# A fused retention and MLP kernel: running state in SBUF, seven products for the first block too, and attention groups taken from a list

## Chip, cores, metric

One core of a Trainium2 chip. The metric is the device time of one execution in microseconds (us), median of the runs; lower is better. The profile's span (first to last instruction) is some 1.5 to 2.5 us shorter than that time. Ratios are the mean time of one kernel's fast runs over the mean of the other's of the same rounds, so they are not quite the ratios of the medians quoted beside them.

## The reference

```python
# q, k, v: (8, 8, 576, 64) float32; w_in: (512, 2048); w_out: (2048, 512)
scores = q @ k^T / sqrt(64)
ret    = scores * gamma_h ** (i - j)   for i >= j, else 0     # gamma_h = 1 - 2**(-5-h)
x      = (ret @ v), heads side by side                        # 4608 tokens x 512
out    = gelu_exact(x @ w_in) @ w_out                         # 4608 x 512, float32
```

## The kernel before

The engines are called as in the profile: PE does the matmuls (PEld its weight loads), DVE elementwise work, ACT copies and GELU, POOL here mostly issues loads. PSUM is the memory, in banks, that PE writes its sums to.

Attention goes by chunks: 8 sequences of 576 tokens, each four chunks of 128 and one of 64 tokens, 40 chunks in all. A chunk is turned (q and k transposed), `scores` gives k·q, DVE masks it, `inner` multiplies by v, `cross` adds what the state of all earlier chunks gives, `evacuate` writes x. The MLP goes by nine blocks of 512 tokens: a first layer (64 matmuls of 512 columns, GELU on ACT) and a second layer.

The program writes its instructions in a fixed order, which a modelled clock picks while the program is built. Each step has a rule for when it is ready; the step placed next is one that is ready by the modelled clock. On the chip each engine then runs its own instructions in that order, and the true semaphores make it wait where the model was wrong.

The second layer of blocks 1 to 8 is done by seven products in place of eight (112 matmuls of 256 columns for the work of 64 of 512). The products need sums of weights (`w_sum`, "T") and sums of g (`s`, "S"), made by DVE. Block 0 does its second layer plainly:

```python
    def mlp2_step(t, ts, m0, m1):              # block 0 only: out rows <- g, w_out tile by tile
        wait(land_out[(m1 - 1) // 2])          # modelled landing of THIS w_out tile
        wait(g_ready(t, ts * 128, ts * 128 + 128, range(m0, m1)))
        ...
    PRODUCTS = {1: ("A11", "B11", "P"), 2: ("A12", "B21", "Q"), 6: ("S2", "T2", "P"), 7: ("S3", "T3", "Q"),
                5: ("S1", "T1", "P"), 3: ("S4", "B22", "P"), 4: ("A22", "T4", "Q")}

    def fast_ready(t, n):                      # when a step of the seven products is ready
        k, p = (LAST_ORDER if t == N_BLK - 1 else FAST_ORDER)[n]
        lhs, rhs, where = PRODUCTS[k]
        ...                                    # sums s or g there, accumulator copied out, a bank free
        if rhs[0] == "T":
            when = max(when, w_sum_end[0])     # nothing is asked for rhs[0] == "B", the plain w_out
        return when

    def state(i):                              # sum over chunks kept in one PSUM bank
        ... matmul(u_ps[0][...], lhsT=k of chunk i, rhs=vh of chunk i, start=(ci == 0 and hp == 0), ...)
        nc.scalar.copy(u, u_ps[0])

    def attend(kind, i):                       # (cut) a pair of chunks: array modes 1, 2, 1
        if len(pend) == 2: state(pend[0])      # mode 1 (128x64)
        for j in pend: inner(j)                # mode 1
        for j in new:  scores(j)               # mode 2 (64x64)
        for j in pend: cross(j)                # mode 2
        if len(pend) == 2: state(pend[1])      # mode 1 again; the MLP's matmuls are mode 0 (128x128)
```

## Time and profile before

| | before |
|---|---|
| time, median of the runs | 298.8 us (298.5 to 299.1) |
| span of the profiled run | 296.9 us |
| PE busy | 288.6 us, 97% |
| DVE / ACT busy | 57% / 44% |
| matmul work done by 35 / 50 us | 19.4 / 33.2 us |

The last row is worked out from the trace: every matmul that has ended, taken at its steady rate (512 columns 0.2158 us, 256 columns 0.1092, 128 columns 0.0558), divided by the tiles that run side by side in its array mode, without warm-up matmuls. The whole program is 262.9 us of this.

Lines of the page of the kernel before: busy time with its share of the span, then PE, DVE and the granted PE clock in 40 slices of 7.4 us (tenths).

```profile
PE 288.6 (97%) x3151; PEld 192.8 (65%) x3151; DVE 169.1 (57%) x368; ACT 130.9 (44%) x259; POOL 113.8 (38%) x146
PE   6999999999999999999999999999999999999995
DVE  4652646947779726986089827581775144402422
PEclk9999999999999999999999999999999999999999
```

PE is busy from the second slice to the last but one, so only less PE work, fewer mode changes or a better start can shorten this. What PE does while the weights are still arriving matters below; this is its timeline there, start and duration in us, then the operation, its shape and count:

```profile
35.48 3.63 PE L435 MATMUL oT<-w_out,g 128*128 128x512 bf16 x16
38.95 0.61 PE L270 MATMUL qk_ps<-ident,qk_ld 128*128 128x128 bf16 x8
39.39 1.03 PE L435 MATMUL oT<-w_out,g 128*128 128x512 bf16 x4
40.35 0.42 PE L295 MATMUL sc<-qkT 64*64 64x128 bf16 x16
40.70 1.90 PE L435 MATMUL oT<-w_out,g 128*128 128x512 bf16 x8
...
43.34 3.63 PE L435 MATMUL oT<-w_out,g 128*128 128x512 bf16 x16
```

From 35 us on PE fills its time with `oT`, block 0's plain second layer.

The cost of a change of array mode is read from the chain of waits, here around one pair of chunks (start, us on the chain, what):

```profile
113.21 0.24 PE u_ps L351 x8
113.45 0.45 PE o_ps L331 x16
113.90 0.35 PE sc L295 x16
114.25 0.45 PE o_ps L370 x16
114.70 0.24 PE u_ps L351 x8
114.94 2.73 PE fast L535 x24
117.67 0.34 PE o_ps L331 x8
118.01 0.12 PE u_ps L351 x8
```

`u_ps x8` is 0.24 us when it opens a group (113.21) or comes behind another mode (114.70), and 0.12 behind `o_ps`, which is in its own mode (118.01): 0.12 us for a change. Walking all matmuls in order of time gives 112 changes.

### The profile page before, as it was taken

To read this page: it belongs to the slowest core of one execution; us is meant where nothing else is said; L and a number is where in the kernel's file an instruction comes from. 1 tells how busy PE (TensorE), PEld (TensorE's weight loads), DVE (VectorE), ACT (ScalarE), POOL (GpSimd) and SP (SyncE) were. 2 spreads that over 40 slices of the span, in tenths; PEclk is the share of its full clock that TensorE was granted. 3 is DMA by queue.
4 is the path that set the end of the run, shared out by engine and by line. 5 is a ranking of instruction groups with operands and counts; after the bars stand their busy time and mean duration, and the time that the engine had idled before them with its cause. 6 is when DMAs were issued, how large, how long until landed. Compare 5 with 4: busy or idle time off the path is not lost.

```text
span 296.9 us, 7431 instructions
## 1 busy us (share of the span) xinstructions
PE 288.6 (97%) x3151; PEld 192.8 (65%) x3151; DVE 169.1 (57%) x368; ACT 130.9 (44%) x259; POOL 113.8 (38%) x146
## 2 busy tenths in 40 slices
PE   6999999999999999999999999999999999999995
PEld 2675755658865488557864786568656864784584
DVE  4652646947779726986089827581775144402422
ACT  4676502655235613554246414651465146426621
POOL 8997879838485260690781075000000000000000
PEclk9999999999999999999999999999999999999999
DMA  9999999999999999999999999900300030003013
GB/s 92 152 182 176 190 187 187 199 144 131 155 147 202 166 155 149 210 157 166 77 230 137 134 78 223 162 10 3 141 2 2 0 143 0 2 5 137 3 35 106
DMA packets 153089, 35.48 MB, mean 119 GB/s; under 512 B 141792, under 2 KB 148960, under 8 KB 153056
## 3 DMA queue, kind: packets, MB, share of 16 engines
q0 software_dynamic: 117872, 18.23, 86.4%
q1 hardware_dynamic: 35184, 16.78, 31.9%
q8 instruction: 24, 0.39, 0.5%
q14 instruction: 9, 0.07, 0.1%
HBM read 36.70 MB, written 9.44 MB: 155 GB/s over the span
## 4 chain that ended last, share of the span: by engine, by line
PE 84%; DMA 7%; DVE 6%; POOL 2%; issue 1%; POOLq 0%; DVEq 0%
PE hT L403 38%; PE fast L535 32%; DMA v_ld<-in_v_dram 4%; PE sc L295 3%; PE o_ps L331 3%; PE o_ps L370 2%; PE oT L435 2%; PE u_ps L351 2%; DMA w_in<-in_moe_w_in_dram 2%; DMA qk_ld<-in_q_dram 1%; PE qk_ps L270 1%; DVE vh L316 1%; POOL qk_ld L185 1%; DVE s L468 1%; DVE qkT L273 1%
## 5 line engine op out<-in xcount | busy, mean ns | idle before, releaser
L403 PE MATMUL hT<-xT,w_in 128*128 128x512 bf16 (+7 forms) x692 | 130.2, 345 | 1.0 <-DVE xT L382 0.8
L409 ACT ACTIVATE g<-hT 128x512 bf16<-128x512 f32 (+6 forms) x173 | 89.5, 527 | 53.7 <-PE hT L403 50.9
L403 PEld LDWEIGHTS <-w_in 128*128 128x128 bf16 x692 | 62.0, 98 | 59.5 <-issue 0.9
L535 PEld LDWEIGHTS <-s 128*128 128x128 bf16 x512 | 49.6, 98 | 7.0 <-DVE s L468 0.8
L185 POOL DMA_DIRECT2D qk_ld<-in_q_dram x39 | 33.9, 869 | 47.1 <-DMA qkT<-qk_ld 39.9
L306 DVE TENSOR_TENSOR ret<-sc,msk 128x512 bf16<-128x512 f32 x64 | 41.1, 682 | 11.1 <-PE sc L295 10.7
L535 PE MATMUL fast<-w_sum,s 128*128 128x256 bf16 x384 | 43.8, 273 | 0.5 <-DVE s L468 0.5
L535 PEld LDWEIGHTS <-g 128*128 128x128 bf16 x384 | 37.5, 98 | 5.8
L185 POOL DMA_DIRECT2D v_ld<-in_v_dram x39 | 34.0, 871 | 12.9 <-DVE s L468 3.5
L559 DVE TENSOR_TENSOR o_sb<-fast,u 128x512 f32<-128x512 f32 (+1 forms) x18 | 11.4, 631 | 48.2 <-PE fast L535 39.2
L185 POOL DMA_DIRECT2D qk_ld<-in_k_dram x39 | 33.9, 869 | 5.6 <-DMA v_ld<-in_v_dram 4.4
L535 PE MATMUL fast<-w_out,g 128*128 128x256 bf16 x256 | 29.3, 273 | 0.0
L382 DVE TENSOR_TENSOR xT<-o_ps,dq 128x512 bf16<-128x512 f32 (+1 forms) x42 | 24.3, 605 | 7.4 <-PE o_ps L370 5.8
L467 DVE TENSOR_TENSOR s<-g 128x512 bf16<-128x512 bf16 x32 | 13.4, 420 | 25.0 <-ACT g L409 24.8
L555 ACT COPY u<-fast 128x512 f32<-128x512 f32 (+1 forms) x18 | 9.7, 538 | 39.9 <-PE fast L535 39.9
L356 ACT CAST u_sb<-u_ps 128x256 bf16<-128x256 f32 x32 | 11.9, 372 | 32.2 <-PE u_ps L351 32.1
L316 DVE TENSOR_TENSOR vh<-v_ld,dv 128x512 bf16<-128x512 bf16 x32 | 21.2, 680 | 6.4 <-DMA v_ld<-in_v_dram 6.4
L535 PE MATMUL fast<-w_out,s 128*128 128x256 bf16 x128 | 15.6, 272 | 0.0
L535 PE MATMUL fast<-w_sum,g 128*128 128x256 bf16 x128 | 15.3, 273 | 0.0
L435 PE MATMUL oT<-w_out,g 128*128 128x512 bf16 x64 | 15.2, 380 | 0.0
L295 PE MATMUL sc<-qkT 64*64 64x128 bf16 (+1 forms) x576 | 14.1, 223 | 0.5 <-ACT qkT L276 0.4
L468 DVE TENSOR_TENSOR s<-s,g 128x512 bf16<-128x512 bf16 x32 | 13.6, 425 | 1.1
(62 smaller groups left out, 192.6 us busy)
## 6 DMA issues: line engine op xcount, KB each, us to landing
out_dram<-o_sb SPq DMA_DIRECT2D x14, 512.0 KB, 4.7
qk_ld<-in_k_dram POOLq DMA_DIRECT2D x32, 128.0 KB, 7.3
v_ld<-in_v_dram POOLq DMA_DIRECT2D x32, 128.0 KB, 7.4
qk_ld<-in_q_dram POOLq DMA_DIRECT2D x31, 128.0 KB, 7.3
w_in<-in_moe_w_in_dram POOLq DMA_DIRECT2D x8, 256.0 KB, 6.8
w_out<-in_moe_w_out_dram POOLq DMA_DIRECT2D x8, 256.0 KB, 7.8
out_dram<-o_sb SPq DMA_DIRECT2D x4, 256.0 KB, 5.8
out_dram<-o_sb SPq DMA_DIRECT2D x8, 128.0 KB, 1.7
```

Of the source, the lines that this page charges most:

```text
L185: nc.gpsimd.dma_start(dst[:cs], src[b, :, c0:c0 + cs, :].rearrange("h s d -> s h d"))
L295: nc.tensor.matmul(sc[e][lo:lo + 64, hp, :cs], lhsT=qkT[sl, 1, hp, lo:lo + 64], rhs=qkT[sl, 0, hp, :cs], start=True, stop=True, skip_group ...
L306: nc.vector.tensor_tensor(r[:cs, :, :cs], sc[e][:cs, :, :cs], msk[:cs, :, :cs].to_broadcast([cs, HP, cs]), op=ALU.mult)
L316: nc.vector.tensor_tensor(vh[:cs], loaded[i][1][:cs], dv[:cs, :, ci:ci + 1].to_broadcast([cs, H, D]), op=ALU.mult)
L356: nc.scalar.copy(u, u_ps[0])
L382: nc.vector.tensor_tensor(xT[:, :, at:at + hi - lo], s["o_ps"][:, :, lo:hi], dq[:, :, c0 + lo:c0 + hi], op=ALU.mult)
L403: nc.tensor.matmul(hT[:, :hi - lo], lhsT=w[:, cc, o:o + 128], rhs=xT[:, cc, tok0 % RING + lo:tok0 % RING + hi], start=(cc == 0), stop=(cc ...
L409: nc.scalar.activation(g_of(t, m, lo, hi), hT[:, :hi - lo], AF.Gelu)
L435: nc.tensor.matmul(oT, lhsT=g_of(t, m, ts * 128, (ts + 1) * 128), rhs=w_out_sb[:, m // 2, m % 2, :], start=(m == 0), stop=(m == N_DF - 1))
L467: nc.vector.tensor_tensor(u[:, 0], a[2, 1], a[2, 2], op=ALU.add)
L468: nc.vector.tensor_tensor(u[:, 1], u[:, 0], a[1, 1], op=ALU.subtract)
L535: nc.tensor.matmul(acc_[:, p, :], lhsT=left(t, lhs, j, p), rhs=right(rhs, j), start=(fresh and j == 0 and (p == 0 or apart)), stop=(j == N ...
```

## The change

Intent: fewer array modes per pair, and one block more by seven products. The state of each chunk is made on its own, two to a bank, and added by DVE to a sum in SBUF, so that both states of a pair can stand in front of `inner` and a pair needs modes 1, 2 and 0. Block 0 goes by seven products; block 1's first layer, which could already be taken beside block 0's second, now goes first where both are ready. How many chunks to start, and when, comes from a list; the load order is another; chunk 9 is turned by DMA and no longer by PE.

```diff
-    N_PE_TR = 10
+    N_PE_TR = 9
+    LOADS = "1 2 i 3 i i 4 i o i i 5 i i 6 7 o o 8 o o o o o"   # digits: chunks, i: w_in, o: w_out
+    PLAN = [(1, 4), (0, 28), (1, 13), (1, 112), (0, 95), (1, 68), (1, 28), (1, 65), (0, 9), (2, 17), ... (0, 29)]
-    FAST_FROM = 1
+    FAST_FROM = 0
-    for what in "1 i 2 i i 3 z i i i i i 4 5 o o o o 6 o o o o 7 8".split():
+    for what in LOADS.split():
 ...
-    def state(i):
+    def states(upto):
+        ... u_ps, tag = bank([128, 2, HP, D], FP32, "u_ps")        # two chunks, each its own sum
+                if ci == 0:            nc.vector.tensor_copy(run_sum, u_ps[:, r])
+                elif ci < NCH - 2:     nc.vector.tensor_tensor(run_sum, run_sum, u_ps[:, r], op=ALU.add)
+                if ci < NCH - 2:       nc.scalar.copy(u, run_sum)
+                else:                  nc.vector.tensor_tensor(u, run_sum, u_ps[:, r], op=ALU.add)
 ...
-    def mlp2_step(t, ts, m0, m1):                  # removed, with its wait for each w_out tile
 ...                                                # fast_ready: still nothing asked for a plain w_out
+    stages = [first_runs[0], first_runs[1] + [second_run[0]], [second_run[0]] + first_runs[1], ...]
 ...
-            if len(pend) == 2: state(pend[0])
+                states(upto)
+                for j in pend: inner(j)
             for j in new: scores(j)
             for j in pend: cross(j)
-            if len(pend) == 2: state(pend[1])
```

More of the change, by code (lines that the diff above doesn't have):

```diff
@@ L54 @@
     N_RING = 4
-    LEAD = 44
-    PAIR_FROM = 2
-    PAIR_LEAD = 70
-    LATE_LEAD = 40
-    FAST_FROM = 1
+    LD_FIX = 2.5
+    LD_TAIL = 1.9
+    T_FIX = 2.4
+    T_TAIL = 4.2
+    T_DMA = 1.8
+    N_DYN = 3
+    LOADS = "1 2 i 3 i i 4 i o i i 5 i i 6 7 o o 8 o o o o o"
+    T_LEAD = 5
+    TR_LEAD = 5
+    PLAN = [(1, 4), (0, 28), (1, 13), (1, 112), (0, 95), (1, 68), (1, 28), (1, 65), (0, 9), (2, 17), (1, 82), (0, 51), (0, 53), (2, 2), (1, 0), (2, 56), (2, 18), (1, 0), (2, 52), (2, 36), (2, 71), (2, 0), (2, 89), (0, 89), (1, 145), (2, 127), (2, 119), (2, 135), (2, 98), (1, 76), (1, 129), (2, 216), (0, 29)]
+    FAST_FROM = 0
     HALF = TOK_BLK // 2
@@ L69 @@
     u_pool = ctx.enter_context(tc.tile_pool(name="u", bufs=4))
-    g_pool = ctx.enter_context(tc.tile_pool(name="g", bufs=1))
+    g_pool = ctx.enter_context(tc.tile_pool(name="g", bufs=2))
     s_pool = ctx.enter_context(tc.tile_pool(name="s", bufs=1))
@@ L99, in on_dve @@
         return on("DVE", ready, n / rate / 960 + 0.072)
-    first = o_pool.tile([128, d_model], FP32, tag="o_std", name="q32", bufs=4).rearrange("p (h d) -> p h d", d=D)
+    first = o_pool.tile([128, d_model], FP32, tag="m1", name="q32").rearrange("p (h d) -> p h d", d=D)
     nc.sync.dma_start(first, q[0, :, 0:C, :].rearrange("h s d -> s h d"))
@@ L135 @@
     nc.vector.memset(ones, 1.0)
+    ret_short = [const_pool.tile([128, HP, 128], BF16, name=f"ret_short{e}") for e in range(2)]
+    vh_short = const_pool.tile([128, H, D], BF16, name="vh_short")
+    for t in ret_short + [vh_short]:
+        nc.vector.memset(t, 0.0)
     diag = const_pool.tile([128, 128], BF16, name="diag")
@@ L159, with serve, transfer, load @@
     nc.scalar.activation(warm_act, ln_scale, AF.Gelu)
-    ret_short = [const_pool.tile([128, HP, 128], BF16, name=f"ret_short{e}") for e in range(2)]
-    vh_short = const_pool.tile([128, H, D], BF16, name="vh_short")
     loaded = {}
-    land_in, land_out = [], []
+    land_in, land_out = [None] * (N_DF // 2), [None] * (N_DF // 2)
     land_q, land_k, land_v = {}, {}, {}
-    dma_clock = [6.0]
-    def land(issue, took):
-        dma_clock[0] = max(dma_clock[0], issue) + took
-        return dma_clock[0]
+    rings = ([], [])
+    dma_at = [0.0]
+    pool_at = [3.3]
+    def serve(queues, t, until, landed):
+        while t < until:
+            heads = [q_[0] for q_ in queues if q_ and q_[0][0] <= t]
+            later = [q_[0][0] for q_ in queues if q_ and q_[0][0] > t]
+            if not heads:
+                if not later:
+                    return
+                t = min(later)
+                continue
+            rate = 1.0 / len(heads)
+            step = min([job[1] / rate for job in heads] + [x - t for x in later] + [until - t])
+            for job in heads:
+                job[1] -= step * rate
+            t += step
+            for q_ in queues:
+                if q_ and q_[0][1] < 1e-9:
+                    _, _, tail, at, key = q_.pop(0)
+                    if landed:
+                        at[key] = t + tail
+    def transfer(ring, start, took, tail, at, key):
+        serve(rings, dma_at[0], clock[0], True)
+        dma_at[0] = max(dma_at[0], clock[0])
+        rings[ring].append([start, took, tail, at, key])
+        ahead = tuple([list(job) for job in q_] for q_ in rings)
+        serve(ahead, dma_at[0], 1e5, True)
+    def load(took, at, key):
+        pool_at[0] = max(pool_at[0], clock[0]) + 0.87
+        transfer(0, pool_at[0] - 0.87 + LD_FIX, took, LD_TAIL, at, key)
     def load_chunk(i, now=0.0):
@@ L185, in load_chunk @@
             nc.gpsimd.dma_start(dst[:cs], src[b, :, c0:c0 + cs, :].rearrange("h s d -> s h d"))
-            at_[i] = land(now + 4.3, 0.88 * cs / C)
+            load(0.87 * cs / C, at_, i)
         loaded[i] = (qk, v_ld)
@@ L199, in load_w_in @@
         w_in_sb.append(t)
-        land_in.append(land(0.0, 1.36))
+        load(1.34, land_in, j)
     def load_w_out():
-        j = len(land_out)
+        j = next(j for j in range(N_DF) if land_out[j] is None)
         nc.gpsimd.dma_start(
@@ L206, in load_w_out @@
         )
-        land_out.append(land(0.0, 1.33))
+        load(1.34, land_out, j)
     load_chunk(0)
-    for what in "1 i 2 i i 3 z i i i i i 4 5 o o o o 6 o o o o 7 8".split():
+    for what in LOADS.split():
         if what == "i":
@@ L214 @@
             load_w_out()
-        elif what == "z":
-            for t in ret_short + [vh_short]:
-                nc.gpsimd.memset(t, 0.0)
         else:
@@ L221 @@
     st = {i: {} for i in range(N_CH)}
-    u_ps = [None]
+    run_sum = const_pool.tile([128, HP, D], FP32, name="run_sum")
     u_free = [0.0]
     mlp_begun = [False]
-    free_at = dict.fromkeys("abcdefg", 0.0)
+    free_at = dict.fromkeys("abcdefgh", 0.0)
     last_tag = [None]
@@ L246, in tiled @@
         if mode[0] != n:
-            clock[0] += 0.1
+            clock[0] += 0.115
         mode[0] = n
@@ L261, in turn @@
                               qk[:cs].rearrange("p j h d -> p (j h d)"), transpose=True)
-            dma_clock[0] = max(dma_clock[0], clock[0] + 3.0) + 1.8 * cs / C
-            s["turned"] = max(clock[0] + 9.0, dma_clock[0] + 1.5)
+            transfer(1, clock[0] + T_FIX, T_DMA * cs / C, T_TAIL, s, "turned")
             return
@@ L335, in inner @@
         s["o_end"] = clock[0] + SEEN
-    def state(i):
-        b, ci, c0, cs = chunks[i]
-        s = st[i]
-        if ci + 1 == NCH:
-            return
-        wait(s["scaled"])
-        wait(u_free[0])
-        tiled(1)
-        if ci == 0:
-            u_ps[0] = ps.tile([128, HP, D], FP32, tag="u", name="u_ps")
-        for hp in range(HP):
-            for e in range(2):
-                h = 2 * hp + e
-                nc.tensor.matmul(u_ps[0][64 * e:64 * e + 64, hp, :], lhsT=loaded[i][0][:cs, 1, h, :],
-                                 rhs=s["vh"][:cs, h, :], start=(ci == 0 and hp == 0),
-                                 stop=(hp == HP - 1), skip_group_check=True)
-        clock[0] += 0.125
-        u = st[i + 1]["u"] = u_pool.tile([128, HP, D], BF16, tag="u", name="u_sb")
-        nc.scalar.copy(u, u_ps[0])
-        u_free[0] = st[i + 1]["u_end"] = on_act(clock[0] + SEEN, 256) + BACK
+    def states(upto):
+        js = []
+        while nxt["U"] <= upto:
+            if chunks[nxt["U"]][1] + 1 < NCH:
+                js.append(nxt["U"])
+            nxt["U"] += 1
+        for n in range(0, len(js), 2):
+            some = js[n:n + 2]
+            for j in some:
+                wait(st[j]["scaled"])
+            tiled(1)
+            u_ps, tag = bank([128, 2, HP, D], FP32, "u_ps")
+            for r, j in enumerate(some):
+                for hp in range(HP):
+                    for e in range(2):
+                        h = 2 * hp + e
+                        nc.tensor.matmul(u_ps[64 * e:64 * e + 64, r, hp, :], lhsT=loaded[j][0][:C, 1, h, :],
+                                         rhs=st[j]["vh"][:C, h, :], start=(r == 0 and hp == 0), stop=(hp == HP - 1),
+                                         skip_group_check=True)
+                clock[0] += 0.125
+            ready = clock[0] + SEEN
+            for r, j in enumerate(some):
+                u = st[j + 1]["u"] = u_pool.tile([128, HP, D], BF16, tag="u", name="u_sb")
+                ci = chunks[j][1]
+                if ci == 0:
+                    nc.vector.tensor_copy(run_sum, u_ps[:, r])
+                    end = on_dve(max(ready, u_free[0]), 256) + BACK
+                elif ci < NCH - 2:
+                    nc.vector.tensor_tensor(run_sum, run_sum, u_ps[:, r], op=ALU.add)
+                    end = on_dve(max(ready, u_free[0]), 256) + BACK
+                if ci < NCH - 2:
+                    nc.scalar.copy(u, run_sum)
+                    u_free[0] = st[j + 1]["u_end"] = on_act(end, 256) + BACK
+                else:
+                    nc.vector.tensor_tensor(u, run_sum, u_ps[:, r], op=ALU.add)
+                    st[j + 1]["u_end"] = end = on_dve(ready, 256) + BACK
+            free_at[tag] = end
@@ L406, in mlp1_step @@
         if (t, m // 4) not in g_tiles:
-            pool, tag_ = (g_pool, "g") if t >= FAST_FROM else (s_pool, "s")
-            g_tiles[t, m // 4] = pool.tile([128, 2, 2, TOK_BLK], BF16, tag=f"{tag_}{m // 4}", name=f"g{m // 4}")
+            g_tiles[t, m // 4] = g_pool.tile([128, 2, 2, TOK_BLK], BF16, tag=f"g{m // 4}", name=f"g{m // 4}")
         nc.scalar.activation(g_of(t, m, lo, hi), hT[:, :hi - lo], AF.Gelu)
@@ L422, in g_ready @@
         return max((g_end.get((t, m, n), 1e6) for m in ms for n in range(lo // 64, hi // 64)), default=0.0)
-    acc, acc_bank = {}, {}
-    def mlp2_step(t, ts, m0, m1):
-        row0 = t * TOK_BLK + ts * 128
-        wait(land_out[(m1 - 1) // 2])
-        wait(g_ready(t, ts * 128, ts * 128 + 128, range(m0, m1)))
-        tiled(0)
-        if m0 == 0:
-            acc[t, ts], acc_bank[t, ts] = bank([128, d_model], FP32, "oT")
-        oT = acc[t, ts]
-        for m in range(m0, m1):
-            nc.tensor.matmul(oT, lhsT=g_of(t, m, ts * 128, (ts + 1) * 128), rhs=w_out_sb[:, m // 2, m % 2, :],
-                             start=(m == 0), stop=(m == N_DF - 1))
-        clock[0] += 0.2163 * (m1 - m0)
-        if m1 == N_DF:
-            o_sb = o_pool.tile([128, d_model], FP32, tag="o_std", name="o_sb", bufs=4)
-            nc.scalar.copy(o_sb, oT)
-            free_at[acc_bank[t, ts]] = on_act(clock[0] + SEEN, 512) + BACK
-            nc.sync.dma_start(out[row0:row0 + 128, :], o_sb)
-            dma_clock[0] = max(dma_clock[0], clock[0]) + 0.6
     w_sum = const_pool.tile([128, 4, N_DF // 2, COL], BF16, name="w_sum")
@@ L455, in sum_weights @@
         for n in range(4):
-            w_sum_end[0] = on_dve(land_out[hi - 1], 256 * (hi - lo), 2) + BACK
-    w_sum_end = [0.0]
+            w_sum_end[lo] = on_dve(land_out[hi - 1], 256 * (hi - lo), 2) + BACK
+    w_sum_end = {0: 1e6, 4: 1e6}
     s_tiles = {}
@@ L513, in fast_ready @@
         if rhs[0] == "T":
-            when = max(when, w_sum_end[0])
+            when = max([when] + list(w_sum_end.values()))
         return when
@@ L569, in store @@
                 nc.sync.dma_start(dst, src)
-                dma_clock[0] = max(dma_clock[0], clock[0]) + 1.2
+                transfer(1, clock[0] + 3.0, 1.3, 2.0, f, "stored")
         if k == 1:
@@ L593, in fast_step @@
             store(1, 0)
-    nxt = {"T": 0, "R": 0, "S": 0, "V": 0}
+    nxt = {"T": 0, "R": 0, "S": 0, "V": 0, "U": 0, "P": 0}
     half = [0]
@@ L600, in tok @@
         return chunks[i][0] * S + chunks[i][2]
+    owner = [i for i in range(N_CH) for _ in range(chunks[i][3] // 64)]
     def x_ready(lo, hi):
-        when = 0.0
-        for i in range(N_CH):
-            if tok(i) < hi and tok(i) + chunks[i][3] > lo:
-                when = max(when, x_at.get(i, 1e6))
-        return when
+        return max([0.0] + [x_at.get(owner[n], 1e6) for n in range(lo // 64, hi // 64)])
     done = {}
@@ L618 @@
     stages = []
-    for t in range(N_BLK):
-        if t < 2:
-            first_runs = [[("d", t, m)] for m in range(N_DF)]
-        else:
-            first_runs = [[("1", t, m, 0, TOK_BLK) for m in range(N_DF)]]
-        if t < FAST_FROM:
-            run = [("2", t, ts, m, m + 2) for m in range(0, N_DF, 2) for ts in range(3)]
-            run += [("2", t, 3, m, m + 4) for m in range(0, N_DF, 4)]
-        else:
-            run = [("s", t, n) for n in range(len(FAST_ORDER))]
-        if t == 0:
-            stages += [first_runs, [run] + [[("d", 1, m)] for m in range(N_DF)]]
-        elif t == 1:
-            stages += [first_runs + [run]]
-        else:
-            stages += [[first_runs[0]], [run]]
+    first_runs = [[[("d", t, m)] for m in range(N_DF)] for t in range(N_DYN)]
+    second_run = [[("s", t, n) for n in range(len(FAST_ORDER))] for t in range(N_BLK)]
+    stages = [first_runs[0], first_runs[1] + [second_run[0]], [second_run[0]] + first_runs[1], [second_run[1]] + (first_runs[2] if N_DYN > 2 else [])]
+    for t in range(2, N_BLK):
+        if t >= N_DYN:
+            stages.append([[("1", t, m, 0, TOK_BLK) for m in range(N_DF)]])
+        elif t > 1:
+            stages.append(first_runs[t])
+        stages.append([second_run[t]])
     paced = [0.0]
@@ L650, in mlp_ready @@
                        free_at[first_free()[0]])
-        if kind == "s":
-            return fast_ready(t, step[2])
-        ts, m0, m1 = step[2:]
-        when = max(land_out[(m1 - 1) // 2], g_ready(t, ts * 128, ts * 128 + 128, range(m0, m1)))
-        return max(when, free_at[first_free()[0]]) if m0 == 0 else when
+        return fast_ready(t, step[2])
     def mlp_pick():
@@ L679, in held, with state_to @@
         return list(range(nxt["S"], nxt["R"]))
+    def state_to(pend, new):
+        return max([-1] + pend[-1:] + ([new[-1] - 1] if new else []))
     def group_ready(pend, new):
         when = max([0.0] + [max(st[i]["masked"], st[i].get("scaled", 1e6)) for i in pend])
-        if pend and chunks[pend[0]][1] > 0:
-            when = max(when, st[pend[0]]["u_end"] - 0.5)
+        for i in pend:
+            if chunks[i][1] > 0:
+                when = max(when, st[i].get("u_end", 0.0) - 0.5)
         when = max([when] + [st[i].get("turned", 1e6) - 0.3 * len(pend) for i in new])
         n = len(pend)
+        for i in range(nxt["U"], state_to(pend, new) + 1):
+            if chunks[i][1] + 1 < NCH:
+                when = max(when, st[i].get("scaled", 1e6))
+                n = len(pend) + 1
         if n:
@@ L689, in group_ready @@
         if new:
-            when = max(when, banks_at(n + 2 * len(new)) - 0.35 * n)
+            when = max(when, banks_at(n + 2 * len(new)) - 0.3 * n)
         return when
@@ L696, in attention_picks @@
         pick = mlp_pick()
-        kind, t = pick[1][0][:2] if pick is not None else ("2", N_BLK)
+        kind, t = pick[1][0][:2] if pick is not None else ("s", N_BLK)
         starved = pick is None or pick[0] > clock[0] + 0.3
-        new = []
-        for j in range(i, min(i + 2, nxt["T"])):
-            if st[j]["turned"] > clock[0] + 4.0:
-                break
-            new.append(j)
-        ahead = 32 * tok(i) / TOK_BLK - paced[0] if i < N_CH else 0.0
-        if t < PAIR_FROM:
-            lead, most = LEAD, 1
-        elif kind == "s":
-            lead, most = LATE_LEAD, 1
-        else:
-            lead, most = PAIR_LEAD, 2
-        if i < N_FIRST or starved:
-            most = 1
-        if ahead > lead:
-            new = []
-        new = new[:most]
-        if most == 2 and len(new) == 1 and i < N_CH - 1:
-            new = []
-        if pend:
-            if new:
-                got.append((group_ready(pend, new), "G", (pend, new)))
-            if not new or starved or (nxt["R"] < N_CH and st[nxt["R"]].get("turned", 1e6) > clock[0] + 2.0):
-                if not (kind in "1s" and t >= PAIR_FROM and nxt["R"] < N_CH) or starved or 32 * tok(pend[0]) / TOK_BLK - paced[0] < 20:
-                    got.append((group_ready(pend, []), "G", (pend, [])))
-        elif new:
-            got.append((group_ready([], new), "G", ([], new)))
+        if nxt["P"] < len(PLAN):
+            size, due = PLAN[nxt["P"]]
+            new = list(range(i, i + size))
+            if (paced[0] >= due or starved) and i + size <= nxt["T"]:
+                got.append((group_ready(pend, new), "G", (pend, new)))
         i = nxt["V"]
-        if i < nxt["T"] and i < nxt["S"] + 4:
+        if i < nxt["T"] and i < nxt["S"] + 5:
             got.append((land_v[i], "V", i))
         i = nxt["T"]
-        if i < N_CH and i in land_v and i <= nxt["S"] + (3 if i < N_PE_TR else 6):
+        if i < N_CH and i in land_v and i <= nxt["S"] + (T_LEAD if i < N_PE_TR else TR_LEAD):
             if i >= N_PE_TR:
@@ L737, in attention_picks @@
                 got.append((max((land_q, land_k)[half[0]][i] + 0.1, banks_at(1)), "T", i))
-        if to_sum:
+        if to_sum and fast_done.get(to_sum[0][0] - 1, 0) >= 12:
             got.append((g_ready(to_sum[0][0], 0, TOK_BLK, range(4 * to_sum[0][1], 4 * to_sum[0][1] + 4)) - 0.1, "Z", 0))
@@ L751, in attend @@
             pend, new = i
-            if len(pend) == 2:
-                state(pend[0])
-            for j in pend:
-                inner(j)
-            if len(pend) == 1:
-                state(pend[0])
+            nxt["P"] += 1
+            upto = state_to(pend, new)
+            if len(pend) == 1 and upto == pend[0]:
+                inner(pend[0])
+                states(upto)
+            else:
+                states(upto)
+                for j in pend:
+                    inner(j)
             for j in new:
@@ L761, in attend @@
                 cross(j)
-            if len(pend) == 2:
-                state(pend[1])
             if new:
@@ L788, in attend @@
             nxt["T"] += 1
+    fast_done = {-1: len(FAST_ORDER)}
     def mlp(run):
@@ L810, in mlp @@
             cost = 1.0
-        elif kind == "s":
+        else:
             fast_step(t, step[2])
+            fast_done[t] = step[2] + 1
             cost = 16 / len(FAST_ORDER)
-        else:
-            mlp2_step(*step[1:])
-            cost = (step[4] - step[3]) / 4
         paced[0] += cost
```

## The prediction

> **What bounds it.** TensorE (PE). The engine table gives PE 288.6 of a 296.9 us span (97%; DVE 57%), the chain of waits runs over PE for 84%, and the list of waits has PE waiting under 5 us, most of it before 12 us. Time is removed by removing matmuls, mode changes and start-up loss, and little else.
>
> **Sizes, from the chain of waits and PE's timeline.** 64 first-layer matmuls of 512 columns take 13.81 us; a second layer by seven products (112 of 256 columns) 12.25; block 0's plain second layer 64 x 0.216 = 13.8. A group of attention matmuls costs 0.11-0.12 us more behind another array mode: u_ps x8 0.12 behind o_ps, 0.24 at the head of a group. The Trainium skill (TensorEngine Tiling, Key Properties) says that a change of tiling mode drains the engine; this trace agrees, with that 0.12. In order of time I count 112 changes, about 13 us. All matmuls at their steady rate are 263 us; the rest is those changes, about 14 us lost before 20 us (loads, and matmuls at half rate, 107 ns per 128 columns, until about 16 us), 3.5 us after the last matmul, and stalls of 0.54 and 0.56 us at 74 and 86 us, where DVE was late: its queue stood behind a v_ld transfer, then made sixteen sums s.
>
> **The change, costed.**
> 1. Block 0 by seven products: 13.8 -> 12.25, -1.6 us on PE.
> 2. A pair needs modes 1, 2, 0, not 1, 2, 1, 0. The list has 33 entries, one empty; about 26 groups with three changes, six with two, and two around the remaining short transpose: about 90, not 112: -2.4 us.
> 3. Chunk 9 is turned by DMA: a short PE transpose with two changes goes, -0.4 us.
> 4. DVE gets 32 copies or additions of 128x256 f32 (0.41 us each, as xT of that shape: 13 us) and block 0's sums and output additions (8 us): about 190 us, 65%. ACT loses 8 copies. Not critical on average: a state is now made a group early, so `cross` doesn't wait for it. But weight sums (5 us), block 0's sums and nine chunks meet between 40 and 60 us, where DVE will be nearly full.
> 5. Loads: w_in begins some 2.5 us later, chunks 2 and 3 earlier, w_out ends last, about 49 us (estimate from 0.87 us per chunk tensor and 1.34 per weight tile). Up to there PE has 27.6 us of first layers and about 11 of attention; before did some 32 in that time. It shouldn't starve, by a thin margin. Start-up: between -2 and +1.5.
> 6. The stalls at 74 and 86 us go (-1); others may come (+1).
>
> Sum: about -5 us of 299.
>
> **Predicted: 294.0 us, 8 in 10 between 290.3 and 297.5.** Faster by over 2% 0.38, within 2% 0.59, slower 0.03.
>
> **What would show it.** No oT group; 1008 fast matmuls, 9 x 12.25 us. Mode changes in PE's timeline 85-97, 0.11-0.12 each. PE's idle time after 20 us as small as before; first hT near 15 us, dense work no later than 20 us. DVE 185-195 us. Tail still 3.5 us.
>
> **What would make it wrong.** PE's order is fixed from a modelled clock, and block 0's first two products check the sums of g but not the arrival of w_out: if PE reaches them before the last w_out tile lands, it stands for microseconds. DVE full between 45 and 60 us would delay the weight sums and so product 6. On the other side, a start-up two or three us better (the load order was surely chosen for that) would pass 2%.

## The result, and the profile after

The changed kernel takes 308.97 us (307.96 to 309.97) against 298.81: ratio 1.0341, 95% interval 1.0304 to 1.0377. It is slower by 3.4%, and outside the predicted range. Executions over 1.5% slower than the fastest of the same kernel are left out of the means.

The same lines of the page after (slices now 7.7 us):

```profile
PE 287.1 (93%) x3217; PEld 200.2 (65%) x3237; DVE 187.2 (61%) x420; ACT 130.5 (42%) x261; POOL 112.5 (37%) x143
PE   6899716999999999999999999999999999999995
DVE  6765904595699869699548395999324453312332
PEclk9999965999999999999999999999999999999999
```

There is a hole in PE in the sixth slice (its digit is 1, near 40 us), DVE falls to 0 with it, and the clock falls to about half. (PE has 3217 matmul records for 3237 weight loads: some records are missing, so its busy time may be a little understated; the lower share comes from the hole.) The list of waits on PE names the hole; its columns are total us, times, longest:

```profile
PE fast L563 <- DMA w_out<-in_moe_w_out_dram: 10.3, 7, 3.5
```

And the timeline of PE shows it, where the kernel before had `oT`:

```profile
35.70 1.03 PE L453 MATMUL hT<-xT,w_in 128*128 128x512 bf16 x4
36.57 0.27 PE L563 MATMUL fast<-w_out,g 128*128 128x256 bf16 x1
38.95 0.27 PE L563 MATMUL fast<-w_out,g 128*128 128x256 bf16 x1 [2.12 <-DMA w_out<-in_moe_w_out_dram]
40.23 0.37 PE L563 MATMUL fast<-w_out,g 128*128 128x256 bf16 x1 [1.01 <-DMA w_out<-in_moe_w_out_dram]
44.06 0.37 PE L563 MATMUL fast<-w_out,g 128*128 128x256 bf16 x1 [3.45 <-DMA w_out<-in_moe_w_out_dram]
...
49.31 0.37 PE L563 MATMUL fast<-w_out,g 128*128 128x256 bf16 x1 [1.03 <-DMA w_out<-in_moe_w_out_dram]
49.48 1.06 PE L303 MATMUL qk_ps<-ident,qk_ld 128*128 128x128 bf16 x8
50.33 2.76 PE L453 MATMUL hT<-xT,w_in 128*128 128x192 bf16 x16
```

Block 0's first product starts at 36.57 us, and each of its eight matmuls needs another w_out tile. The last tile lands at 49.3 us. Everything behind it on PE waits, ready or not: the transposes of the next chunk and block 1's first layer run only from 49.5 us.

The windows of the trace give the granted clock beside it (stretch in us; its length; busy us and counts of PE, PEld, DVE, ACT, POOL; then clock, DMA share, GB/s):

```profile
38.00:40.00 2.00, 0.27 (x1) 0.10 (x1) 0.35 (x1) 0.00 (x0) 1.58 (x3) 1.00 1.84 176
40.00:44.00 4.00, 0.37 (x1) 0.10 (x1) 0.00 (x0) 0.00 (x0) 2.76 (x4) 0.51 1.70 188
51.00:53.00 2.00, 2.00 (x14) 1.59 (x11) 1.97 (x5) 0.99 (x3) 2.00 (x3) 0.50 2.39 159
54.00:58.00 4.00, 4.00 (x61) 3.82 (x53) 3.09 (x6) 2.77 (x9) 4.00 (x6) 1.00 2.01 176
```

The clock is halved just after 40 us and stays halved until 53.7, over four us into dense work: `fast` takes 0.37 us for 256 columns there and 0.27 elsewhere.

Everything else came much as costed: 90 mode changes, DVE 187.2 us, no `oT`, the tail after the last matmul near 3 us. PE had done 18.1 us of matmul work by 35 us (before: 19.4) but 20.8 by 50 us (before: 33.2). (Two missing records there are worth 0.4 us.)

The missing question for a plain w_out was in the rule of the kernel before too. It did no harm there: the first product was placed at 69.6 us, long after w_out had landed.

### The profile page after: what moved, and what is told of

The parts are those of the page before. It is cut to its first block, busy times and chain, and to the rows that moved or that the text cites. A ratio compares the mean times of both kernels' runs of the same rounds, so it can differ in the third digit from the quotient of the medians.

```text
span 307.1 us, 7604 instructions
## 1 busy us (share of the span) xinstructions
PE 287.1 (93%) x3217; PEld 200.2 (65%) x3237; DVE 187.2 (61%) x420; ACT 130.5 (42%) x261; POOL 112.5 (37%) x143
## 4 chain that ended last, share of the span: by engine, by line
PE 82%; DMA 10%; POOL 5%; issue 1%; DVE 1%; POOLq 0%; DVEq 0%
PE hT L453 37%; PE fast L563 36%; DMA w_out<-in_moe_w_out_dram 5%; DMA w_in<-in_moe_w_in_dram 5%; PE sc L328 3%; POOL qk_ld L222 2%; PE o_ps L364 2%; PE o_ps L420 2%; PE u_ps L387 2%; POOL v_ld L222 1%; POOL w_in L233 1%; PE qk_ps L303 0%; DVE ret L339 0%; POOL qk_ld L111 0%; POOL v_ld L114 0%
## 5 line engine op out<-in xcount | busy, mean ns | idle before, releaser
L453 PE MATMUL hT<-xT,w_in 128*128 128x512 bf16 (+6 forms) x713 | 129.6, 335 | 1.9 <-DMA w_in<-in_moe_w_in_dram 0.5
L453 PEld LDWEIGHTS <-w_in 128*128 128x128 bf16 x732 | 66.4, 99 | 57.5 <-DMA w_in<-in_moe_w_in_dram 1.3
L563 PEld LDWEIGHTS <-s 128*128 128x128 bf16 x576 | 55.8, 98 | 6.9
L563 PEld LDWEIGHTS <-g 128*128 128x128 bf16 x432 | 41.6, 98 | 17.4 <-issue 10.7
L563 PE MATMUL fast<-w_sum,s 128*128 128x256 bf16 x432 | 49.2, 273 | 0.0
L563 PE MATMUL fast<-w_out,g 128*128 128x256 bf16 x288 | 35.7, 275 | 10.3 <-DMA w_out<-in_moe_w_out_dram 10.3
L495 DVE TENSOR_TENSOR s<-g 128x512 bf16<-128x512 bf16 x36 | 15.1, 420 | 35.8 <-ACT g L458 35.1
L402 ACT CAST u_sb<-run_sum 128x256 bf16<-128x256 f32 x24 | 9.7, 405 | 25.2 <-DVE run_sum L399 19.1
L563 PE MATMUL fast<-w_sum,g 128*128 128x256 bf16 x144 | 17.2, 273 | 0.0
L306 DVE COPY qkT<-qk_ps 128x512 bf16<-128x512 bf16 (+1 forms) x12 | 4.4, 398 | 17.6 <-PE qk_ps L303 17.6
L497 DVE TENSOR_TENSOR s<-g 128x512 bf16<-128x512 bf16 x36 | 15.0, 418 | 0.0
```

What stands on the lines that cost most here:

```text
L453: nc.tensor.matmul(hT[:, :hi - lo], lhsT=w[:, cc, o:o + 128], rhs=xT[:, cc, tok0 % RING + lo:tok0 % RING + hi], start=(cc == 0), stop=(cc ...
L495: nc.vector.tensor_tensor(u[:, 0], a[2, 1], a[2, 2], op=ALU.add)
L497: nc.vector.tensor_tensor(u[:, 2], a[1, 1], a[2, 1], op=ALU.subtract)
L563: nc.tensor.matmul(acc_[:, p, :], lhsT=left(t, lhs, j, p), rhs=right(rhs, j), start=(fresh and j == 0 and (p == 0 or apart)), stop=(j == N ...
```

## The experiments

The theory: the loss is one wait in the wrong place. PE runs its matmuls in order, the two first products of block 0 were placed with nothing asked about w_out, and behind them stood work that was ready; the half clock behind the hole is added to it. Rivals: (a) the later loads starve PE, whatever the order; (b) the three modes are worth nothing; (c) block 0 by seven products costs more than it saves; (d) the running sum's load on DVE costs what PE gains.

| run | time, us (median of the fast runs) | before beside it | ratio to before, 95% interval |
|---|---|---|---|
| after, as given | 308.97 | 298.81 | 1.0341 (1.0304 to 1.0377) |
| e1 readiness asks for w_out | 297.27 | 299.72 | 0.9913 (0.9862 to 0.9965) |
| e2 hole filled with zeros | 306.90 | 299.72 | 1.0239 (1.0198 to 1.0281) |
| e3 e1 with more mode changes | 300.25 | 299.72 | 1.0021 (0.9982 to 1.0061) |
| e4 before, with seven products in block 0 alone | 305.29 | 299.72 | 1.0187 (1.0146 to 1.0228) |
| e5 e1 again | 297.24 | 299.38 | 0.9939 (0.9906 to 0.9972) |
| e6 e1 with block 0 plain | 299.03 | 299.38 | 0.9999 (0.9956 to 1.0042) |
| e7 e1 with 32 DVE copies more | 299.27 | 299.38 | 0.9998 (0.9970 to 1.0025) |
| e8 e1, other loads and list | 296.31 | 299.38 | 0.9892 (0.9860 to 0.9924) |
| e9 e1, ten copies on ACT | 297.47 | 298.88 | 0.9943 (0.9912 to 0.9973) |
| e10 e1, second other list | 298.73 | 298.88 | 0.9986 (0.9950 to 1.0021) |
| e11 e1, third other list | 297.52 | 298.88 | 0.9957 (0.9922 to 0.9991) |

All gave correct results.

### e1: ask for w_out

```diff
         if rhs[0] == "T":
             when = max([when] + list(w_sum_end.values()))
+        if rhs[0] == "B":
+            when = max([when] + list(land_out))
         return when
```

> The changed kernel, with one line added: block 0's first two products are not placed on PE before the modelled landing of the last w_out tile. Theory (PE blocked in order behind w_out): the 10.3 us of waiting for w_out goes, and so does the stretch at half clock behind it (4.4 us of matmuls at half rate, about 2.2 us); 309.0 - 12.5 = 296.5 us, 0.992 of before; at most 1 us of waiting for w_out left; clock 1.00 from about 10 us on. Rival (the later loads starve PE whatever the order): the idle time only moves to waits for x or w_in or the weight sums between 36 and 60 us, time stays at 303 us or more.

Measured: 297.27 us, 0.9913 of before; no wait for w_out is left in the list of waits, and the clock is 1.00. Windows of e1:

```profile
20.00:35.00 15.00, 14.71 (x164) 8.70 (x164) 9.63 (x23) 8.41 (x20) 11.94 (x15) 1.00 1.88 178
35.00:50.00 15.00, 13.63 (x247) 11.32 (x246) 14.24 (x32) 7.79 (x25) 10.93 (x15) 1.00 1.71 185
```

Between 35 and 50 us PE runs 247 matmuls where the changed kernel ran 41, and does 11.5 us of matmul work (18.1 to 29.6) in place of 2.7. The matmuls and loads are the same; only their order differs. Rival (a) falls as the cause of the slowdown: 11.7 us by the medians, 4.3% of before by the ratios, came from two lines of a rule. What e1 still lacks against the predicted 294 is taken up in e7 to e11.

### e2: keep PE busy while it waits

```diff
+        if (t, n) == (0, 0):
+            filler = ps.tile([128, 512], FP32, tag=first_free()[0], name="warm")
         for j in range(N_DF // 2):
+            for _ in range((0, 9, 4, 15, 4, 4, 4, 5)[j] if (t, n) == (0, 0) else 0):
+                nc.tensor.matmul(filler, lhsT=zeros[:, :128], rhs=zeros, start=True, stop=True)
             nc.tensor.matmul(acc_[:, p, :], lhsT=left(t, lhs, j, p), rhs=right(rhs, j), ...
```

> The changed kernel with its order kept, and 45 matmuls of zeros put between the eight that wait for w_out, so that PE is not idle while it waits. Result as before. If the half clock behind the stall costs time of its own: clock 1.00 through 40 to 54 us, last of the eight matmuls still near 49.3 us, and 309.0 - 2.2 = 306.8 us (0.993 of the changed kernel). If the clock costs nothing: 309 us.

Measured: 306.90 us. The wait has the same length, as PE's timeline shows; the stretch behind it now runs at full clock:

```profile
48.40 1.24 PE L566 MATMUL warm<-zeros 128*128 128x512 bf16 x5
49.57 0.27 PE L567 MATMUL fast<-w_out,g 128*128 128x256 bf16 x1
49.70 0.61 PE L303 MATMUL qk_ps<-ident,qk_ld 128*128 128x128 bf16 x8
50.14 1.48 PE L453 MATMUL hT<-xT,w_in 128*128 128x192 bf16 x16
```

The 16 `hT` of 192 columns take 1.48 us where they took 2.76. So the half clock was worth 2.1 us by the medians (3 by the ratios, taken in different rounds), and the order the rest. Note what this page would say to a careless reader: PE busy 97%, as before, in a kernel that stands still for ten us.

### e3: put mode changes back

```diff
                 states(upto)
-                for j in pend:
-                    inner(j)
             for j in new:
                 scores(j)
+            if not (len(pend) == 1 and upto == pend[0]):
+                for j in pend:
+                    inner(j)
             for j in pend:
                 cross(j)
```

> e1 with the inner products of a group placed behind the scores: modes 1, 2, 1, 2 in place of 1, 2, so two changes of mode more in some 20 to 26 groups and not one matmul more. Theory (a change costs 0.11 to 0.12 us of PE): 40 to 52 changes more, 4.5 to 6 us slower than e1. Rival (the drains hide behind other waits, so that the 22 changes that the change saves are worth nothing): within 1 us of e1.

Measured: 300.25 us, 3.0 us more than e1 in the same rounds. The walk through its matmuls counts 122 changes, 32 more than e1's 90 (I had expected 40 to 52, because I counted groups too generously); that is 0.093 us a change by the medians; the ranges of the four runs of each leave 0.07 to 0.13, so the 0.11 to 0.12 of the chain is not refuted. A group of it on the chain of waits:

```profile
128.60 0.37 PE u_ps L387 x16
128.97 0.47 PE sc L328 x24
129.44 0.57 PE o_ps L364 x16
130.01 0.56 PE o_ps L420 x16
```

`o_ps L364 x16` is 0.57 us here behind another mode, 0.45 in the chain of before behind its own. Rival (b) falls: the 22 changes that the change saves are worth about 22 x 0.093 = 2.0 us (1.5 to 2.9 by those ranges).

### e4: seven products in block 0, alone, in the kernel before

```diff
-    FAST_FROM = 1
+    FAST_FROM = 0
-    g_pool = ctx.enter_context(tc.tile_pool(name="g", bufs=1))
+    g_pool = ctx.enter_context(tc.tile_pool(name="g", bufs=2))
...
         if rhs[0] == "T":
-            when = max(when, w_sum_end[0])
+            when = max(when, w_sum_end[0] if not weights_due else 1e6)
+        if rhs[0] == "B":
+            when = max([when] + list(land_out))
...
-        if to_sum:
+        if to_sum and fast_done.get(to_sum[0][0] - 1, 0) >= 12:
```

> The kernel before with block 0 by seven products alone (g in two buffers, weight sums and sums of g for block 0, products wait for all of w_out); load order, states and groups as before. If the 1.6 us of matmuls are what it is worth: 297.3 us, 0.995 of before. If block 0's plain second layer was also what PE did while w_out was still arriving (it takes w_out tile by tile, the products need all of it and its sums): PE waits between 35 and 56 us, and the time is 301 to 306 us, slower than before.

Measured: 305.29 us, 1.0187. PE's timeline where `oT` had been:

```profile
36.89 0.40 PE L270 MATMUL qk_ps<-ident,qk_ld 128*128 128x128 bf16 x4 [0.65 <-DMA qk_ld<-in_q_dram]
38.48 0.40 PE L270 MATMUL qk_ps<-ident,qk_ld 128*128 128x128 bf16 x4 [1.19 <-DMA qk_ld<-in_k_dram]
41.06 2.08 PE L403 MATMUL hT<-xT,w_in 128*128 128x192 bf16 x12 [2.19 <-DVE xT L382]
```

The window of that stretch, to be laid beside that of e1 (13.63 us busy at a clock of 1.00):

```profile
35.00:50.00 15.00, 10.48 (x119) 8.57 (x120) 9.15 (x22) 3.95 (x12) 11.71 (x15) 0.77 1.99 172
```

The 1.6 us of matmuls saved are real, and 5.6 us of time are lost. Part of the loss is again the clock, which is halved here from 40.2 to 47.0 us (mean 0.77 in the window): about 3 us by an estimate from some 6 us of matmuls that ran in it at half rate. The rest is waiting, of two kinds. The short waits (0.65 and 1.19 us) are for q and k of the next chunk, which the old load order brings no earlier. The longest one, 2.19 us, is not for loads: block 1's first layer (`hT` of 192 columns) stood beside the products here as well, and the x that it needed had been ready to copy since 36.1 us, when PE had done its `o_ps`. But DVE made twelve of block 0's sums first, from 35.9 to 40.3 us, and the copy `xT` stood behind them in order: the fault of the changed kernel again, on another engine. So e4 shows that block 0 by seven products can't be put in by itself: the plain layer was work that could be done with part of w_out, seven products need all of it, and their sums get in the way of other work. How much each of these costs, and whether the old load order alone would forbid the change, is not shown.

### e5: e1 once more

No edit.

> The kernel of e1 once more, as the base of the three beside it and for a narrower interval: 0.991 of before, between 0.988 and 0.994.

Measured: 297.24 us, 0.9939. The two runs of e1 together leave it faster than before by 0.6 to 0.9%, which is within the 2% that counts as the same.

### e6: block 0 plain again, in e1

```diff
+    second_run[0][:] = [("2", 0, ts, m, m + 2) for m in range(0, N_DF, 2) for ts in range(3)]
+    second_run[0] += [("2", 0, 3, m, m + 4) for m in range(0, N_DF, 4)]
...                                              # and mlp2_step with its readiness, as in the kernel before
```

> The kernel of e1 with block 0's second layer plain again (64 matmuls of 512 columns that take w_out tile by tile as it lands), all else as in e1. Matmuls alone: 1.6 us slower than e1. If the plain layer, which can start before all of w_out is there, also fills the 1.4 us that PE idles in e1 between 35 and 50 us, the two cancel: within 0.7 us of e1. Rival (seven products in block 0 are what costs, by their sums and waits): faster than e1 by over 1 us.

Measured: 299.03 us over four fast runs (298.17 to 301.34); two more, 302.80 and 303.34 us, are slow. The ratio of 0.9999 against e5's 0.9939 in the same rounds makes it about 1.8 us slower than e1's kernel, with intervals that just overlap. That is near the 1.6 us of the matmuls alone, and the rival (over 1 us faster) did not come; but the trace shows that more than the matmuls moved. As expected, PE has no idle time between 35 and 50 us (15.00 of 15 busy, e1: 13.63). But the list of waits has a new one, PE for DVE's sums `s`, 3.3 us in two waits: DVE stood 7.7 us in front of a scaling of v (`vh`) that waited for its load, with block 1's sums behind it in order. So the total says nothing clean about (c); the order was fitted to the other kernel. That seven products in block 0 hurt once the order is right is not shown; the matmul sum and the fast runs speak against it.

### e7: 32 operations more on DVE, in e1

```diff
                 ci = chunks[j][1]
+                nc.vector.tensor_copy(u, u_ps[:, r])
                 if ci == 0:
                     nc.vector.tensor_copy(run_sum, u_ps[:, r])
```

> The kernel of e1 with each state copied once more by DVE before it is added to the running sum (the copy is then overwritten; the result stays right): 32 operations of about 0.41 us, 13 us of DVE more, as much as the running sum itself added. If DVE's load is off the critical path, as predicted: within 1 us of e1, and DVE busy near 200 us. If the running sum's load is what e1 still lacks against the predicted 294: 2 us or more slower.

Measured: 299.27 us, 2.0 us more than e5 in the same rounds; DVE busy 197.4. Its windows to be laid beside those of e1:

```profile
20.00:35.00 15.00, 14.30 (x183) 9.05 (x184) 9.51 (x23) 8.47 (x24) 12.01 (x16) 1.00 1.87 178
35.00:50.00 15.00, 12.98 (x227) 10.10 (x225) 14.68 (x34) 7.78 (x23) 11.05 (x15) 1.00 1.70 185
```

By 50 us it has done 28.2 us of matmul work and e5 30.2; it is 2.7 behind at 55 us and 2.9 at 200 us. So the loss lies in the start, and later the extra load costs next to nothing. It is not tied to the stretch where DVE is full, though (35 to 50 us: 14.68 of 15 us; e1 14.24; the kernel before 6.76): at 35 us e7 has done 17.0 us and is already 1.1 behind e1 and 1.7 behind e5, with DVE busy 9.51 of the 15 us before, and between 35 and 50 us it loses only 0.3 more. Its list of waits has 2.1 us of `hT` waiting for DVE's xT, e1's 0.7. So how full DVE is does not tell the loss; which operation PE is waiting for does. The "not critical on average" of the prediction holds after 60 us and not before. How much of this the running sum itself costs isn't measured: the extra copies also lengthen the path from state to `u`.

### e8, e10, e11: other lists and load orders, in e1

```diff
-    LOADS = "1 2 i 3 i i 4 i o i i 5 i i 6 7 o o 8 o o o o o"
+    LOADS = "1 2 i i i 3 i i 4 5 i 6 i i o o o o 7 8 o o o o"      # e8
-    PLAN = [(1, 4), (0, 28), ...]
+    PLAN = [(2, 218), (1, 49), (1, 89), (2, 65), ...]              # e8: 26 entries
```

> The kernel of e1 with another order of loads (w_in earlier, w_out in a block) and another list of groups (26 entries), chosen after the check was in the rule that places the products. If e1's missing 2 us lie in a list and a load order that were fitted to a rule with the fault in it: 1 to 2 us faster than e1, some 295.5 us, about 0.987 of before, with fewer than 90 mode changes. Rival (start-up is bound by the loads themselves): within 0.6 us of e1.

> The kernel of e1 with a second other load order and list, chosen with DVE's operations taken 6% longer. As e8: if the list and order were what e1 lacked, 0.985 to 0.988 of before; if start-up is bound by the loads, within 0.6 us of e1 (0.992).

> A third list and load order, otherwise as e10. Same expectation: 0.985 to 0.988 of before, or 0.992.

Measured: 0.9892, 0.9986 and 0.9957. e8 is the fastest kernel, 296.31 us, with 80 mode changes; e10 and e11 (e11 with 83 changes) are no faster than e1. e10 shows new waits of about 2 us each, for DVE and for a transposing DMA. All three had been chosen as better by the modelled clock; on the chip they lie within 1% of each other on both sides of e1, so it does not rank lists that finely. e8 beats both kernels of the study, but by 1.1% (before) and not by over 2%; against e5 in the same rounds it is 0.9 us faster by the medians and 1.4 by the ratios, about what was expected. In three of its six runs the mean clock is 0.993 or 0.994 and the time 296.9 us on the mean, in the other three 1.00 and 295.4 us; in the profiled one, of the first kind, the clock is halved from 19.4 to 22.8 us. So this list seems to lose over 1 us more in those runs that get a halved clock in the start, which the modelled clock knows nothing of.

### e9: ten copies from DVE to ACT, in e1

```diff
-                nc.vector.tensor_copy(qkT[:, j, :, :cs], ps_[:, :, :cs])
+                (nc.vector.tensor_copy if i == 0 else nc.scalar.copy)(qkT[:, j, :, :cs], ps_[:, :, :cs])
```

> The kernel of e1 with its order unchanged, and the ten PSUM copies of turned q and k of chunks 4 to 8 (0.40 us each, nearly 4 us between 20 and 60 us) moved from DVE to ACT. In e1 DVE is busy 13.7 to 14.2 of the 15 us between 35 and 50 us (6.8 of 15 in the kernel before), and PE idles 1.4 us there. If DVE's load in the start is what e1 lacks: PE's idle time between 35 and 50 us falls from 1.4 us to 0.7 or less, and the time by 0.5 to 1 us. Rival (the order and the loads are what lacks, and DVE is merely full): within 0.3 us of e1, or slower because ACT then holds up g.

Measured: 297.47 us, 0.9943, against 0.9939 for e5 (other rounds). PE's busy time between 35 and 50 us rose to 14.30 of 15, so the idle time fell to 0.70 us as expected, and the time did not move. In its profiled run 1.1 us of waiting for `s` stands behind 50 us (e1 had 0.8 of it in one profiled run and none in the other). The first half of the expectation held, the second did not; but the gain was not given back there: at 100 us, before that wait (107 us), it had done 77.6 us of matmul work, e1 77.1 and e5 77.7, so it was not ahead of e1's own scatter. Where the gain went is open.

## Why the prediction was wrong, point by point

- **"It shouldn't starve, by a thin margin" (point 5): this is the step that failed.** I compared amounts: 27.6 us of first layers and 11 of attention against the 32 us that PE had done by then. The amount was there: e1 does 11.5 us of it between 35 and 50 us. But it stood behind a product that could not run. The list of waits has 10.3 us there, and the half clock adds 2.1 (e2). Removing the cause alone takes 309.0 to 297.3 us (e1).
- I had read the missing question and named it, with its consequence, under "What would make it wrong", and gave "slower" 0.03. The fault of method is that it was left as a risk. The rule could be followed through by hand: block 0's g is complete once its first layer ends (36 us in the trace), w_out at 49 us by my own estimate, and the readiness rule had nothing else to hold the product back. That is a wait of about 12 us in the expected case, not in a tail.
- **Seven products, -1.6 us (point 1).** The matmul sum falls as costed (262.9 to 261.1 us with chunk 9's transpose). Alone it costs 5.6 us (e4), with about 3 of it at half clock: where the plain layer had used w_out piece by piece, PE waited for loads and for a copy that stood behind the new sums on DVE. I took a sum of matmul time for a saving without asking what PE would do in its place.
- **Mode changes, -2.4 us (point 2).** The count was right, 112 to 90. The price from end to end was 0.093 us by the medians (e3), so about -2.0; the runs' ranges do not exclude the 0.11.
- **DVE "not critical on average" (point 4).** The total was right (187.2 us), and so was the warning that the start is different; what was missing was a price for it. 32 operations more cost 2.0 us, nearly all of it before 60 us, and about half of that before 35 us, earlier than the 40 to 60 us that I had named (e7).
- **Start-up between -2 and +1.5 us.** Even in e1 PE is 3.0 to 3.6 us of matmul work behind the kernel before at 50 us (29.6 and 30.2 against 33.2). With -1.8 for matmuls, -2.0 for modes and -1.1 for the two stalls of before, that leaves about -1.3 to -1.9, and e1 is 2.1 to 2.5 us faster by the medians. The sum closes roughly. Which part of those 3 us is DVE, which the order of loads and which the list stays open: e7 shows that DVE's load matters there, e9 that taking some of it away brought nothing, e8 that another order can win about 1 us.

## What to carry to other kernels

An engine that runs in order pays for one early placement with everything behind it; so when a change moves an operation to an earlier place, list all its operands and ask of each when it lands, even where the old code never had to ask. A cheaper algorithm that needs all of its inputs can lose to a dearer one that takes them piece by piece, as long as they are still being loaded (e4 points that way, with other causes mixed in). And a risk that you can name and follow through by hand belongs into the expected value, not into the list of what might go wrong.

## What the Trainium skill lacked or had wrong

- "TensorE: Matmul & The Clock Gate", "Why this matters for your kernels", warns of idle gaps over about 3 us between bursts. This case agrees in the effect, not in the threshold as that row has it: the clock was halved at 40.1 us although the two gaps up to there were 2.12 and 1.01 us, with one matmul of 0.27 us between. In e4 it was halved at 40.2 us, after gaps of 0.65 and 1.19 us and 1.3 us into a third. Too little work in a stretch was enough. The full clock came back at 53.7 us, 4.3 us after dense work began at 49.5, which agrees with the 4 us, give or take 0.5, that Part 1 of the page states. The page does not say that matmuls of zeros keep the clock up; e2 shows that they do (1.00 throughout).
- The same page, Part 3, "The mechanism", says that matmuls stay in strict order and only weight loads are pulled ahead. This case agrees: nothing behind the blocked product ran from 36.8 to 49.3 us, and e1 ran 11.5 us of it. No page that I used draws the consequence for placing work while weights are still landing.
- "TensorEngine Tiling (Array Packing)", "Key Properties", says that a change of tiling mode drains the engine, and gives no cost. Here it is 0.11 to 0.12 us on the chain of waits, and 0.093 us each from end to end (32 changes, 3.0 us; 0.07 to 0.13 by the runs' ranges).
- "Trainium Kernel Development and Optimization", "Performance Expectations", calls matmul busy time a bad metric and names two in its place, MFU and the busy share of weight loads. e2 is a case of the first: 97% busy, in a kernel 2.4% slower than one that is 97% busy too. The busy share of weight loads (65% before, 67% in e2) doesn't show the loss either. MFU was not worked out here; the count of matmul work done by a given time, which is close to it in kind, shows the loss and where it lies.
